# A third quad of half-size products in one batch's second MLP product, and a new order of the instructions around it

## The chip, the core and the metric

The kernel runs on one core of one Trainium2 chip. The time is the device time of one launch, in microseconds (us). One core has five engines that matter here, each with its own queue, worked off in order: TensorE for matmuls (PE in the profile), VectorE (DVE), ScalarE (ACT), GpSimd (POOL) and SyncE (SP), which issues most DMAs. Matmul results land in PSUM, in eight banks of 512 float32 for each partition; the other operands lie in SBUF.

## The reference, cut to what matters

Block-sparse attention over 4 batches, 8 heads, 768 tokens and 64 columns a head, then a residual MLP over x (4 x 768 x 512):

```
scores = q @ k.T / 8, masked by 32x32 blocks;  x = softmax(scores) @ v      # heads side by side: 512 columns
tok = w_tok @ (alpha1 * x + beta1);             u = x + lam * tok
a2 = alpha2 * u + beta2
out = u + lam * (relu(a2 @ w_ch1) @ w_ch2)      # w_ch1 512 x 2048, w_ch2 2048 x 512
```

The change concerns the last product, h = relu(a2 @ w_ch1) times w_ch2, of batch 2 alone.

## The kernel before

Pairs of heads are numbered 0 to 15, four to a batch. Each pair goes through nine score units, three of which form a **group of scores**. For a unit, PE makes the scores (`emit_qk`, matmul at L601), ACT takes the exponential (L619), DVE multiplies by the mask (`emit_keep`, L636, in the text "a mask product"), and PE multiplies by v (L671 or L648, in the text a "pv": 12 small matmuls). When a head is complete, DVE divides (L688 the reciprocal, L689 the product) into x_sb, and the two affine instructions of `emit_a1pp` (L705, L706) follow on POOL, for the last head of a batch and the last two of all on DVE.

Between these, the work of the MLPs is woven in. The order is written out by hand in strings: `W1`, `W2`, `W2L` and `W3` (L43 on; `W2L` begins at L68), one row for each group of scores, one letter for each job, and `token` (L1460) emits what a letter stands for. Instructions reach their engines' queues in that order. The letters needed here:

- q: the scores of the group's three units and the first exponential; x: the next exponential; k: a mask product; p: a pv; s: the head pair's follow-up work is made ready; Y: v is copied for the next pair.
- f: one of 32 pieces of batch 2's first MLP product (`job_f1`): four matmuls of 384 columns at L919 into a PSUM bank, then ACT's relu (L926) into hts. hts holds tokens in two chunks, tiles 0 to 2 and tiles 3 to 5.
- g: a job of the second product, from the list `P_ORDER[2]` (L1287). There are two kinds. **Direct** (`job_f2`): a tile of 128 tokens takes four jobs of four matmuls of 512 columns (L1058), then a sum into x_sb on DVE (L1067) and a store. **Quad** (`job_p`, L1187): two tiles of tokens go together and are multiplied by Strassen's scheme in Winograd's form: seven products, P1 to P7, of eight matmuls of 256 columns each (L1170), each followed by a sum into x_sb on DVE (`plus`, L1180).
- S: one of the four sums of halves of hts that a quad needs (`job_s`, L1144, a DVE instruction of 128 x 1024 bfloat16). P6 needs the second, P5 the first, P7 the third, P3 the fourth.
- W: one of eight sums of quarters of w_ch1 (`job_w`, L974, DVE), which batch 3's first product uses after all the attention. They are written into the buffer in which batch 1's output lay.
- T: a third of the token product (`job_tok2`): twelve matmuls of 256 columns at L846, a sum on DVE (L858), two casts (L865). d: a DMA transpose; v: an affine on ACT (L887); D: sums for batch 3's first product (L989).

In a quad, P1, P6 and P5 add up in one PSUM bank, and DVE takes the bank's contents into x_sb after each of the three; P7 and P4 share another bank in the same way; P2 and P3 have a bank each. PSUM is shared out by tag: `mm_tile` (L469) has three banks, `sp_tile` two pairs and `op_tile` one. A pair of `mm` banks goes to the first score unit of every group, one to every f, every T, every direct tile, and to P2, P7 and P3. P1 takes a half of an `sp` pair. A new tile takes a bank whose last user stands earlier in the written order, and its first matmul waits until that user is done.

Before the change batch 2 has two direct tiles (0 and 3) and two quads, (1, 4) and (2, 5). `W2L` has 12 rows, the attention of batch 3, pairs 12 to 15; below, "row 10" is its tenth string. Rows 6 to 12 are those that the change rewrites. `W3` follows: its first row ends pair 15 (three pvs), goes on with quad jobs and then the three T of pairs 14 and 15.

Of the kernel before, what the change touches and what calls it, by code (L numbers as in the profile page):

```python
# [18 lines left out]
B = 4  # L19
H = 8  # L20
S = 768
# [4 lines left out]
DM = 512  # L26
P = 128
NT = S // P
# [52 lines left out]
]  # L81
W3 = [
# [6 lines left out]
HN = NH // 2  # L89
# [159 lines left out]
def kernel(  # L249
# [16 lines left out]
    nc = tc.nc  # L266
# [194 lines left out]
    def sp_tile():  # L461
        return psum.tile([P, 2, 512], FP, name="sp", tag="sp", bufs=2)
# [111 lines left out]
    x_sbs = {}  # L574
# [234 lines left out]
    did = set()  # L809
# [3 lines left out]
    hts = {}  # L813
# [256 lines left out]
    def emit_store(b, o, sl, eng=nc.sync):  # L1070
        eng.dma_start(
            out[b].rearrange("(p o) n -> p o n", o=NT)[:, o, sl], x_sbs[b][:, o, sl]
        )
# [41 lines left out]
    def a_of(b, t, name, r=slice(0, HN)):  # L1115
        if name in ("X1", "X2"):
            return xs[(b, t, name)][:, r]
        c, half = {"11": (0, 0), "12": (0, 1), "21": (1, 0), "22": (1, 1)}[name]
        return hts[(b, c)][:, HN * half + r.start : HN * half + r.stop, ts(t, P)]

    SOP = {
        1: ("X1", "21", "22", ALU.add),
# [5 lines left out]
    def job_s(b, t, n, r=slice(0, HN)):  # L1128
        dst, a, c, op = SOP[n]
        rows = range(r.start, r.stop)  # L1130
        for name in (a, c):
            if name[0] == "X":
                assert all(("S", b, t, int(name[1]), m) in did for m in rows)
            else:
                h, half = divmod(int(name) - 11, 10)
                assert all(("f", b, h, HN * half + m) in did for m in rows)
# [19 lines left out]
        7: ("21", "T3", 3),  # L1156
    }
    banks = {}

    def mul(b, t, n, ps, start, cols=slice(0, HC)):  # L1160
        a, m, need = PROD[n]
        assert m in bq or all((m, r) in did for r in range(0, HN, 2))
        if need:
            assert all(("S", b, t, need, r) in did for r in range(HN))
        c, half = {"1": (0, 0), "X": (1, 0)}.get(a[0], (1, 0))
        if need == 0:
            h, half = divmod(int(a) - 11, 10)
            assert all(("f", b, h, HN * half + r) in did for r in range(HN))
        for r in range(HN):
            nc.tensor.matmul(  # L1170
                ps,
                a_of(b, t, a)[:, r],
                b_rows(m, r)[:, 0, cols],
                start=(start and r == 0),
                stop=(r == HN - 1),
                skip_group_check=True,
            )

    def plus(x, ps):
        nc.vector.tensor_tensor(out=x, in0=x, in1=ps, op=ALU.add)  # L1180

    def twice(ps):
        return ps.unsqueeze(1).broadcast_to([P, 2, HC])

    lo, hi = slice(0, HC), slice(HC, DM)

    def job_p(b, t, n):  # L1187
        x = x_sbs[b]
        last = (b, t) == (B - 1, NT // 2 - 1)
        bk = banks.setdefault((b, t), {})  # L1190
        if n in (1, 2, 7):
            bk[n] = sp_tile()[:, 0] if n == 1 else mm_tile()[:]
        if n == 3 and not last and 2 not in bk:
            bk[2] = mm_tile()[:]
        if n == 1:
            mul(b, t, 1, bk[1][:, lo], True)
            plus(x[:, t, lo], bk[1][:, lo])
        elif n == 2:
            mul(b, t, 2, bk[2][:, lo], True)
            if last or b < B - 1:  # L1200
                plus(x[:, t, lo], bk.pop(2)[:, lo])
            if last:
                emit_store(b, t, lo)
        elif n == 6:
            mul(b, t, 6, bk[1][:, lo], False)
            plus(x[:, t + 3, lo], bk[1][:, lo])
        elif n == 7:
            mul(b, t, 7, bk[7][:, lo], True)
            plus(x[:, t + 3, hi], bk[7][:, lo])
        elif n == 5:  # L1210
            mul(b, t, 5, bk[1][:, lo], False)
            plus(x[:, t : t + 4 : 3, hi], twice(bk[1][:, lo]))
        elif n == 4:
            mul(b, t, 4, bk[7][:, lo], False)
            plus(x[:, t + 3, lo], bk[7][:, lo])
            emit_store(b, t + 3, slice(0, DM))
        elif last:
            for h in range(2):
                sl = slice(HC + h * P, HC + h * P + P)
                ps = (mm_tile(), op_tile([P, DM]))[h]  # L1220
                mul(b, t, 3, ps[:, sl], True, ts(h, P))
                plus(x[:, t, sl], ps[:, sl])
                emit_store(b, t, sl, (nc.sync, nc.scalar)[h])
        else:
            sl = hi if b < B - 1 else slice(0, DM)
            mul(b, t, 3, bk[2][:, hi], b < B - 1)
            plus(x[:, t, sl], bk[2][:, sl])
            emit_store(b, t, slice(0, DM))
        did.add((b, t, n))

    NPAIR = B * NP
# [34 lines left out]
    def start_mlp(b):  # L1266
        if b == B - 1:
            todo["f"] += [
                lambda j=j: job_m(*j) if len(j) == 2 else job_f1(*j) for j in last_f1()
            ]  # L1270
        else:
            todo["f"] += [
                lambda c=c, n=n: job_f1(b, c, n) for c in range(2) for n in range(NH)
            ]
        if b not in STR:
            todo["g"] += [
                lambda o=o, g=g: job_f2(b, o, g) for o in range(NT) for g in range(4)
            ]
# [5 lines left out]
        todo["S"] += [lambda t=t, n=n, r=r: job_s(b, t, n, r) for t, n, r in S_ORDER[b]]  # L1284

    REST = (6, 7, 5, 4, 3)
    P_ORDER = {  # L1287
        2: [(0, g, "g") for g in range(4)]
        + [(t, 2) for t in (1, 2)]
        + [(3, g, "g") for g in range(4)]  # L1290
        + [(t, 1) for t in (1, 2)]
        + [(t, n) for t in (1, 2) for n in REST],
        3: [(t, n) for t in range(2) for n in (1, 2)]
        + [(t, n) for t in range(2) for n in REST]
        + [(2, n) for n in (1, 2) + REST],
    }
    ALL, R1, R2 = slice(0, HN), slice(0, HN // 2), slice(HN // 2, HN)
    S_ORDER = {
        2: [(t, n, ALL) for t in (1, 2) for n in (1, 2, 3, 4)],
        3: [(t, n, R1) for n in (1, 2, 3) for t in range(3)]  # L1300
        + [(t, n, r) for t in range(3) for n, r in ((1, R2), (2, R2), (3, R2), (4, ALL))],
    }

    def start_pair(i):
# [227 lines left out]
```

## Time and profile before

| what | us |
|---|---|
| median of 3 runs (lowest to highest) | 298.71 (298.64 to 299.35) |
| the profiled execution, whole | 298.76 |
| its span in the profile | 297.1 |
| what lies around the span | 1.66 |
| PE busy | 289.7 |
| DVE busy | 237.8 |
| ACT busy | 217.1 |
| POOL busy | 109.8 |

The granted clock of TensorE was 1.00 of full speed over the span. The profile's page gives busy times and the costliest groups of instructions. The trace answers further views: the chain of work that ended last, followed back from the last instruction and listed in order of time (start, length, engine and line); the timeline of an engine, in which "x3" means three instructions merged into one entry; and windows, which give each engine's busy time in a stretch. The ends of matmuls are modelled and overlap the next one's start, so that a matmul's price is read from start to start or from the chain, not from its own length.

### The profile page before, as it was taken

To read this page: it belongs to the slowest core of one execution; us is meant where nothing else is said; L and a number is where in the kernel's file an instruction comes from. 1 tells how busy PE (TensorE), PEld (TensorE's weight loads), DVE (VectorE), ACT (ScalarE), POOL (GpSimd) and SP (SyncE) were. 2 spreads that over 40 slices of the span, in tenths; PEclk is the share of its full clock that TensorE was granted. 3 is DMA by queue.
4 is the path that set the end of the run, shared out by engine and by line. 5 is a ranking of instruction groups with operands and counts; after the bars stand their busy time and mean duration, and the time that the engine had idled before them with its cause. 6 is when DMAs were issued, how large, how long until landed. Compare 5 with 4: busy or idle time off the path is not lost.

```text
span 297.1 us, 7554 instructions
## 1 busy us (share of the span) xinstructions
PE 289.7 (98%) x3082; PEld 193.5 (65%) x3101; DVE 237.8 (80%) x485; ACT 217.1 (73%) x324; POOL 109.8 (37%) x149
## 2 busy tenths in 40 slices
PE   8999999999999999999999999999999999999995
PEld 3688888665567565565576466556576679665884
DVE  4988899995678796977878777895956899799774
ACT  4999999998899963999779581999869744576000
POOL 8997978632443710355323340335320300000000
PEclk9999999999999999999999999999999999999999
DMA  6999999992392995729955767745520211400032
GB/s 182 184 199 186 192 171 187 171 123 44 95 147 55 112 203 84 118 65 119 125 96 73 124 110 146 103 92 69 70 62 17 38 38 29 141 1 3 0 141 73
DMA packets 57274, 31.09 MB, mean 105 GB/s; under 512 B 37204, under 2 KB 54016, under 8 KB 57240
## 3 DMA queue, kind: packets, MB, share of 16 engines
q0 software_dynamic: 16752, 14.22, 34.4%
q1 hardware_dynamic: 40020, 15.92, 29.3%
q8 instruction: 24, 0.39, 0.6%
q10 hardware_dynamic: 468, 0.47, 0.5%
q14 instruction: 10, 0.08, 0.1%
HBM read 29.75 MB, written 6.29 MB: 121 GB/s over the span
## 4 chain that ended last, share of the span: by engine, by line
PE 84%; DVE 6%; DMA 4%; ACT 3%; issue 1%; POOL 1%; SPq 0%; POOLq 0%
PE mm L919 18%; PE mm L1058 13%; PE sp L601 10%; PE mm L846 8%; PE op L671 7%; PE mm L1170 5%; PE sp L1170 4%; PE mm L601 3%; DVE eT L636 3%; PE mm L822 3%; PE op L648 2%; DMA vr<-in_v_dram 2%; ACT eT L619 2%; PE mm L1016 2%; PE sp L1016 2%; DMA uraw<-ubf 2%
## 5 line engine op out<-in xcount | busy, mean ns | idle before, releaser
L619 ACT ACTIVATE eT<-sp,expb 128x1024 f16<-128x1024 f32 x111 | 118.4, 1120 | 2.1 <-PE sp L601 1.4
L636 DVE TENSOR_TENSOR eT<-eT,mask 128x1024 f16<-128x1024 f16 x99 | 80.6, 843 | 13.5 <-ACT eT L619 13.3
L919 PE MATMUL mm<-uT,w1b 128*128 128x384 bf16 x416 | 76.8, 326 | 0.4 <-ACT hts L926 0.3
L705 POOL TENSOR_TENSOR a1pp<-x_sb,vbc 128x384 bf16<-128x384 f32 x25 | 28.5, 1138 | 119.0 <-DVE x_sb L689 84.7
L619 ACT ACTIVATE eT<-mm,expb 128x512 f16<-128x512 f32 x66 | 41.7, 685 | 26.5 <-PE mm L601 26.3
L926 ACT ACTIVATE hts<-mm 128x384 bf16<-128x384 f32 x104 | 49.1, 502 | 13.3 <-PE mm L919 12.4
L919 PEld LDWEIGHTS <-w1b 128*128 128x128 bf16 x416 | 38.7, 98 | 26.4 <-issue 2.9
L1058 PE MATMUL mm<-w2b,hts 128*128 128x512 bf16 x205 | 52.2, 379 | 0.9 <-issue 0.2
L671 PEld LDWEIGHTS <-eT 128*128 128x128 f16 x792 | 29.8, 98 | 8.8 <-issue 1.7
L1058 PEld LDWEIGHTS <-hts 128*128 128x128 bf16 x224 | 19.8, 98 | 22.3 <-issue 3.9
L671 PE MATMUL op<-vext,eT 128*128 128x65 f16 x792 | 32.1, 194 | 0.4 <-DVE x_sb L689 0.3
L601 PE MATMUL sp<-qTs,kTs 88*128 88x512 bf16 (+1 forms) x120 | 26.9, 325 | 1.2 <-ACT eT L619 0.7
L706 POOL TENSOR_TENSOR a1pp<-a1pp,vbc 128x384 bf16<-128x384 bf16 x25 | 26.7, 1069 | 2.0
L846 PE MATMUL mm<-a1pp,wtokT 128*128 128x256 bf16 x216 | 25.9, 273 | 0.1
L846 PEld LDWEIGHTS <-wtokT 128*128 128x128 bf16 x216 | 20.6, 98 | 5.6 <-issue 1.8
L1170 PEld LDWEIGHTS <-hts 128*128 128x128 bf16 x208 | 19.5, 98 | 3.0 <-issue 0.3
L858 DVE TENSOR_TENSOR x_sb<-x_sb,mm 128x512 f32<-128x512 f32 x18 | 12.3, 686 | 9.9 <-PE mm L846 9.8
L601 PE MATMUL sp<-qhT,khT 64*128 64x256 bf16 (+1 forms) x176 | 19.8, 322 | 0.0
L601 PEld LDWEIGHTS <-khT 64*128 64x128 bf16 x264 | 10.6, 94 | 12.7 <-issue 9.2
L648 PEld LDWEIGHTS <-eT 128*128 128x128 f16 x360 | 14.9, 97 | 3.8 <-issue 0.3
L689 DVE TENSOR_TENSOR x_sb<-op,rcp 128x384 f32<-128x384 f32 x28 | 15.6, 558 | 1.0
L1067 DVE TENSOR_TENSOR x_sb<-x_sb,mm 128x512 f32<-128x512 f32 x14 | 9.6, 686 | 8.2 <-PE mm L1058 6.7
(135 smaller groups left out, 376.9 us busy)
## 6 DMA issues: line engine op xcount, KB each, us to landing
out_dram<-x_sb SPq DMA_DIRECT2D x23, 256.0 KB
qpad<-in_q_dram POOLq DMA_DIRECT2D x15, 192.0 KB, 4.6
kr<-in_k_dram POOLq DMA_DIRECT2D x15, 192.0 KB, 5.3
vr<-in_v_dram POOLq DMA_DIRECT2D x15, 192.0 KB, 6.3
w1b<-in_moe_w_ch_dram POOLq DMA_DIRECT2D x4, 512.0 KB, 9.2
w2b<-in_moe_w_ch_dram POOLq DMA_DIRECT2D x4, 512.0 KB, 7.7
hts<-in_moe_w_tok_dram POOLq DMA_DIRECT2D x2, 576.0 KB, 8.7
x_sb<-in_k_dram ACTq DMA_DIRECT2D x2, 192.0 KB
```

The lines of the kernel that those rows point to most:

```text
L601: nc.tensor.matmul(sp[jj][:, dst], lhsT, rhs, start=True, stop=True, skip_group_check=True,)
L619: nc.scalar.activation(dst, at, AF.Exp, bias=expb[:], scale=SCALE)
L636: nc.vector.tensor_mul(out=e, in0=e, in1=keep)
L648: nc.tensor.matmul(op[0][:, o, :], ets[u][:, jj, h * QB + n * P : h * QB + n * P + P], vexts[i % NVB][:, w, 2 * jp + jj, :], start=op[1] == 0,
L671: nc.tensor.matmul(op[0][:, o, :], ets[u][:, jj, h * QB + n * P : h * QB + n * P + P], vexts[i % NVB][:, w, 2 * jp + jj, :], start=op[1] == 0,
L705: eng.tensor_tensor(out=dst, in0=x_sbs[b][:, :, cols], in1=bc[0], op=ALU.mult)
L706: eng.tensor_tensor(out=dst, in0=dst, in1=bc[1], op=ALU.add)
L846: nc.tensor.matmul(ps[:, o], wtokT[:, os_, ts(2 * n + o, P)], a1pps[i][:, os_, :], start=(os_ == 0 and o == 0), stop=(os_ == NT - 1 and o ...
L919: nc.tensor.matmul(ps[:, 0:QC], w1b[:, dk, ts(n, P)], uTs[b][:, dk, ts(c, QC)], start=(dk == 0), stop=(dk == 3),)
L926: nc.scalar.activation(h_row(b, c, n), ps[:, 0:QC], AF.Relu)
L1058: nc.tensor.matmul(ps[:], ht[:, nk, ts(o % 3, P)], w2b[:, nk, :], start=(nk == 0), stop=(nk == NH - 1),)
L1170: nc.tensor.matmul(ps, a_of(b, t, a)[:, r], b_rows(m, r)[:, 0, cols], start=(start and r == 0), stop=(r == HN - 1), skip_group_check=True,)
```

## The change

Batch 2's second product now has no direct tile. Its six tiles form three quads: (0, 1), whose tokens both lie in the first chunk of hts, (2, 5) and (3, 4). A quad is named by its two tiles, and `a_of`, `job_s` and `job_p` read the tiles from the name; batch 3's quads keep their pairs (t, t + 3). In the first quad, P1 takes one of the three `mm` banks, no longer half an `sp` pair, and the bank stays in use through P6 and P5, which stand in later places: P2 at the end of row 9, P1 and P6 in row 10, P5, P7 and P3 in row 11, P4 in row 12. The f's move up: at the end of row 9 one is left, where there were five before. The S's of quad (0, 1) stand in rows 7, 8 and 10 (two), those of (2, 5) in rows 11, 12 and `W3`, those of (3, 4) in `W3`. Of the W's, five move into row 6; three stay in row 7. `W3` is not changed; its g's and S's now belong to quads (2, 5) and (3, 4).

```diff
-    "q k 0 f x f p s f f x 1 L p k 2 f f f k Y f",
-    "q f L f 0 f k W W W W W W W W 1 f Y x f p g x f p f g k k 2",
-    "q x k x k Q 0 g 1 s f f g p 2 p f f k p f",
-    "q T 0 k f 1 x k f T x f 2 p k K p f",
-    "q x 0 x T k 1 k f 2 k f Q f d p L",
-    "q x 0 x K k g d k s f g f 1 k p p S S g 2",
-    "q p Y x x k g k S 0 1 k 2 g v g v g",
+    "q k 0 f x f p s f f x 1 L p k W W 2 f f f k Y W W W f",
+    "q f L f 0 f k W W W 1 f f S Y x f p f x f p f f k k 2",
+    "q x f k x f k Q 0 1 s f f p 2 p f f k S p f",
+    "q T 0 k f 1 x k f T x f 2 p k K p g",
+    "q S S g x 0 x T k g 1 k f 2 k g Q d p L",
+    "q x g 0 x K k d g k s f 1 k p p g S S 2",
+    "q p Y x x k g k S 0 1 k 2 g v g v",
...
-        c, half = {"11": (0, 0), "12": (0, 1), "21": (1, 0), "22": (1, 1)}[name]
-        return hts[(b, c)][:, HN * half + r.start : HN * half + r.stop, ts(t, P)]
+        o, half = t[int(name[0]) - 1], int(name[1]) - 1
+        return hts[(b, o // 3)][:, HN * half + r.start : HN * half + r.stop, ts(o % 3, P)]
...
+    LATE = [(2, (2, 5)), (2, (3, 4))] + [(3, (o, o + 3)) for o in range(3)]
...
     def job_p(b, t, n):
-        x = x_sbs[b]
+        x, (o1, o2) = x_sbs[b], t
...
-        if n in (1, 2, 7):
-            bk[n] = sp_tile()[:, 0] if n == 1 else mm_tile()[:]
+        if n == 1 and (b, t) in LATE:
+            bk[1] = sp_tile()[:, 0]
+        elif n in (1, 2, 7) or (n == 3 and not tail):
+            bk[n] = mm_tile()[:]
...
-        2: [(0, g, "g") for g in range(4)]
-        + [(t, 2) for t in (1, 2)]
-        + [(3, g, "g") for g in range(4)]
-        + [(t, 1) for t in (1, 2)]
-        + [(t, n) for t in (1, 2) for n in REST],
+        2: quad((0, 1), (2, 1, 6))
+        + quad((2, 5), (2,))
+        + quad((0, 1), (5, 7, 3, 4))
+        + quad((3, 4), (2,))
+        + quad((2, 5), (1,))
+        + quad((3, 4), (1,))
+        + quad((2, 5), REST)
+        + quad((3, 4), REST),
...
-        2: [(t, n, ALL) for t in (1, 2) for n in (1, 2, 3, 4)],
+        2: [(t, n, ALL) for t in ((0, 1), (2, 5), (3, 4)) for n in (1, 2, 3, 4)],
```

More of the change, by code (lines that the diff above doesn't have):

```diff
@@ L1117, in a_of, with a_ready @@
             return xs[(b, t, name)][:, r]
-        c, half = {"11": (0, 0), "12": (0, 1), "21": (1, 0), "22": (1, 1)}[name]
-        return hts[(b, c)][:, HN * half + r.start : HN * half + r.stop, ts(t, P)]
+        o, half = t[int(name[0]) - 1], int(name[1]) - 1
+        return hts[(b, o // 3)][:, HN * half + r.start : HN * half + r.stop, ts(o % 3, P)]
+    def a_ready(b, t, name, rows):
+        if name[0] == "X":
+            return all(("S", b, t, int(name[1]), m) in did for m in rows)
+        o, half = t[int(name[0]) - 1], int(name[1]) - 1
+        return all(("f", b, o // 3, HN * half + m) in did for m in rows)
     SOP = {
@@ L1130, in job_s @@
         rows = range(r.start, r.stop)
[L1131 to L1136, printed above, removed]
+        assert a_ready(b, t, a, rows) and a_ready(b, t, c, rows)
         if n == 3:
@@ L1164, in mul @@
             assert all(("S", b, t, need, r) in did for r in range(HN))
[L1165 to L1168, printed above, removed]
+        assert a_ready(b, t, a, range(HN))
         for r in range(HN):
@@ L1187, in job_p @@
     def job_p(b, t, n):
-        x = x_sbs[b]
-        last = (b, t) == (B - 1, NT // 2 - 1)
+        x, (o1, o2) = x_sbs[b], t
+        tail = b == B - 1
+        last = tail and o2 == NT - 1
         bk = banks.setdefault((b, t), {})
-        if n in (1, 2, 7):
-            bk[n] = sp_tile()[:, 0] if n == 1 else mm_tile()[:]
-        if n == 3 and not last and 2 not in bk:
-            bk[2] = mm_tile()[:]
+        if n == 1 and (b, t) in LATE:
+            bk[1] = sp_tile()[:, 0]
+        elif n in (1, 2, 7) or (n == 3 and not tail):
+            bk[n] = mm_tile()[:]
         if n == 1:
             mul(b, t, 1, bk[1][:, lo], True)
-            plus(x[:, t, lo], bk[1][:, lo])
+            plus(x[:, o1, lo], bk[1][:, lo])
         elif n == 2:
             mul(b, t, 2, bk[2][:, lo], True)
-            if last or b < B - 1:
-                plus(x[:, t, lo], bk.pop(2)[:, lo])
+            if last or not tail:
+                plus(x[:, o1, lo], bk[2][:, lo])
             if last:
-                emit_store(b, t, lo)
+                emit_store(b, o1, lo)
         elif n == 6:
             mul(b, t, 6, bk[1][:, lo], False)
-            plus(x[:, t + 3, lo], bk[1][:, lo])
+            plus(x[:, o2, lo], bk[1][:, lo])
         elif n == 7:
             mul(b, t, 7, bk[7][:, lo], True)
-            plus(x[:, t + 3, hi], bk[7][:, lo])
+            plus(x[:, o2, hi], bk[7][:, lo])
         elif n == 5:
             mul(b, t, 5, bk[1][:, lo], False)
-            plus(x[:, t : t + 4 : 3, hi], twice(bk[1][:, lo]))
+            plus(x[:, o1 : o2 + 1 : o2 - o1, hi], twice(bk[1][:, lo]))
         elif n == 4:
+            assert {(b, t, m) for m in (5, 6, 7)} <= did
             mul(b, t, 4, bk[7][:, lo], False)
-            plus(x[:, t + 3, lo], bk[7][:, lo])
-            emit_store(b, t + 3, slice(0, DM))
+            plus(x[:, o2, lo], bk[7][:, lo])
+            emit_store(b, o2, slice(0, DM))
         elif last:
@@ L1221, in job_p @@
                 mul(b, t, 3, ps[:, sl], True, ts(h, P))
-                plus(x[:, t, sl], ps[:, sl])
-                emit_store(b, t, sl, (nc.sync, nc.scalar)[h])
-        else:
[L1225 to L1228, printed above, removed]
+                plus(x[:, o1, sl], ps[:, sl])
+                emit_store(b, o1, sl, (nc.sync, nc.scalar)[h])
+        else:
+            assert {(b, t, m) for m in (1, 2, 5)} <= did
+            sl, ps = (slice(0, DM), bk[2]) if tail else (hi, bk[3])
+            mul(b, t, 3, ps[:, hi], not tail)
+            plus(x[:, o1, sl], ps[:, sl])
+            emit_store(b, o1, slice(0, DM))
         did.add((b, t, n))
@@ L1284, in start_mlp, with direct, quad @@
         todo["S"] += [lambda t=t, n=n, r=r: job_s(b, t, n, r) for t, n, r in S_ORDER[b]]
+    def direct(*tiles):
+        return [(o, g, "g") for o in tiles for g in range(4)]
+    def quad(t, order):
+        return [(t, n) for n in order]
     REST = (6, 7, 5, 4, 3)
     P_ORDER = {
-        2: [(0, g, "g") for g in range(4)]
-        + [(t, 2) for t in (1, 2)]
-        + [(3, g, "g") for g in range(4)]
-        + [(t, 1) for t in (1, 2)]
-        + [(t, n) for t in (1, 2) for n in REST],
-        3: [(t, n) for t in range(2) for n in (1, 2)]
-        + [(t, n) for t in range(2) for n in REST]
-        + [(2, n) for n in (1, 2) + REST],
+        2: quad((0, 1), (2, 1, 6))
[6 more added lines that the diff above has]
+        + quad((3, 4), REST),
+        3: quad((0, 3), (1, 2))
+        + quad((1, 4), (1, 2))
+        + quad((0, 3), REST)
+        + quad((1, 4), REST)
+        + quad((2, 5), (1, 2) + REST),
     }
     ALL, R1, R2 = slice(0, HN), slice(0, HN // 2), slice(HN // 2, HN)
+    Q3 = [(0, 3), (1, 4), (2, 5)]
     S_ORDER = {
-        2: [(t, n, ALL) for t in (1, 2) for n in (1, 2, 3, 4)],
-        3: [(t, n, R1) for n in (1, 2, 3) for t in range(3)]
-        + [(t, n, r) for t in range(3) for n, r in ((1, R2), (2, R2), (3, R2), (4, ALL))],
+        2: [(t, n, ALL) for t in ((0, 1), (2, 5), (3, 4)) for n in (1, 2, 3, 4)],
+        3: [(t, n, R1) for n in (1, 2, 3) for t in Q3]
+        + [(t, n, r) for t in Q3 for n, r in ((1, R2), (2, R2), (3, R2), (4, ALL))],
     }
```

## Prediction

> **What bounds the kernel now.** I read the page first, for the busy shares and the chain.
>
> ```profile
> PE 289.7 (98%) x3082; PEld 193.5 (65%) x3101; DVE 237.8 (80%) x485; ACT 217.1 (73%) x324; POOL 109.8 (37%) x149
> PE 84%; DVE 6%; DMA 4%; ACT 3%; issue 1%; POOL 1%; SPq 0%; POOLq 0%
> ```
>
> PE is busy 98% of the span and carries 84% of the chain, so matmul time that goes is time won, unless another engine sets the pace in the stretch where it goes. The next view is the windows, cut where the groups of scores of rows 10, 11 and 12 begin and where the first T of `W3` begins.
>
> ```profile
> core 0: us, PE busy (x) PEld busy (x) DVE busy (x) ACT busy (x) POOL busy (x), PEclk, DMA share, GB/s
> 225.25:229.70 4.45, 4.45 (x45) 3.03 (x46) 2.22 (x5) 4.43 (x8) 0.00 (x0) 1.00 0.02 4
> 229.70:235.58 5.88, 5.71 (x62) 3.88 (x64) 5.63 (x10) 4.52 (x7) 2.24 (x2) 1.00 0.34 66
> 235.58:244.07 8.49, 8.41 (x101) 5.94 (x100) 7.80 (x17) 5.10 (x6) 0.00 (x0) 1.00 0.09 33
> 244.07:255.50 11.43, 11.43 (x107) 10.24 (x108) 10.54 (x23) 4.16 (x8) 0.00 (x0) 1.00 0.23 65
> ```
>
> The second number of a row is the window's length, the third PE's busy time. In rows 11 and 12 DVE is busy 5.63 of 5.88 and 7.80 of 8.49: nearly as full as PE. The chain says the same.
>
> ```profile
> 232.78 0.34 DVE x_sb L1180
> 233.13 0.04 issue
> 233.17 0.81 PE mm L919 x4
> ...
> 236.84 0.21 DVE rcp L688
> ...
> 243.46 0.57 DVE a1pp L706
> 244.03 0.05 issue
> 244.07 4.11 PE mm L846 x36
> ```
>
> At 233.17 an f starts only when DVE has emptied the bank that it takes (a `plus` that ended at 233.12): the three `mm` banks already tie PE to DVE here. At 244.07 the first T of `W3` starts when DVE's last a1pp is done. From 236.84 to there the chain runs on DVE alone, one instruction after another, 7.23 us. After 244.07 PE is busy without a gap.
>
> **The price of the matmuls**, from other pieces of the chain, where PE runs back to back:
>
> ```profile
> 181.43 1.31 PE mm L846 x12
> 182.74 1.73 PE mm L1058 x8
> ...
> 197.13 0.43 PE sp L601 x4
> ...
> 198.97 0.36 PE op L671 x12
> ...
> 248.18 0.87 PE sp L1170 x8
> ...
> 269.04 0.65 PE mm L919 x4
> ```
>
> A T is 1.31, a pv 0.36, an f 0.65, a quad's product 0.87, a job of a direct tile half of 1.73. The scores of a group are 0.76 (the four of 0.43 and some 0.33 for the rest). The change removes two direct tiles, 2 x 4 x 0.865 = 6.92, and adds 7 x 0.87 = 6.10: **0.82 less on PE**. In rows 6 to 9 the work stays the same (four direct jobs go, 3.46; four f's and P2 come, 2.60 + 0.87), so the whole 0.82 is in rows 10 to 12. The Trainium skill, page "TensorE: Matmul & The Clock Gate", section "Back-to-back issue gap", gives a sustained 131 ns for a matmul of 512 columns and 81 ns for 128; with some 98 ns for 256 in between, an estimate, the direct tiles would cost 4.2 and the quad 5.5, and the change would lose 1.3 on PE. The rows above (216 and 109 ns) fit that section's other formula, N/2.4 + 2.5 ns, and so speak for the 0.82.
>
> **What it puts on DVE.** Four sums S (0.68 each), seven plus instead of two: about 3.8 us more before 244, in a queue that is nearly full there. To see what is late, I follow PE and DVE through rows 10 to 12 in the new order. These rows give the starts and the steps:
>
> ```profile
> 225.17 0.39 PE L601 MATMUL mm<-qhT,khT 64*128 64x512 bf16 x2
> 225.92 1.48 PE L846 MATMUL mm<-a1pp,wtokT 128*128 128x256 bf16 x12
> 229.66 0.46 PE L601 MATMUL mm<-qhT,khT 64*128 64x512 bf16 x2
> 235.51 0.39 PE L601 MATMUL mm<-qhT,khT 64*128 64x256 bf16 x4
> ```
>
> ```profile
> 227.44 0.69 DVE L858 TENSOR_TENSOR x_sb<-x_sb,mm 128x512 f32<-128x512 f32 x1 [2.22 <-PE mm L846]
> ...
> 228.58 1.89 DVE L636 TENSOR_TENSOR eT<-eT,mask 128x1024 f16<-128x1024 f16 x3
> ...
> 230.61 0.56 DVE L689 TENSOR_TENSOR x_sb<-op,rcp 128x384 f32<-128x384 f32 x1
> 231.38 1.41 DVE L636 TENSOR_TENSOR eT<-eT,mask 128x1024 f16<-128x1024 f16 x1 [0.21 <-ACT eT L619]
> 232.71 0.41 DVE L1180 TENSOR_TENSOR x_sb<-x_sb,mm 128x256 f32<-128x256 f32 x1
> 233.04 1.07 DVE L636 TENSOR_TENSOR eT<-eT,mask 128x1024 f16<-128x1024 f16 x1
> ```
>
> A T that starts at 225.92 ends at 227.23; DVE starts its sum 0.21 later, and with its two casts needs 1.14 (227.44 to 228.58). A mask product costs 0.60 from start to start (three in 1.89, the last 0.69 long), a plus 0.33 (232.71 to 233.04; 0.41 till it ends), the plus of P5, over 512 columns, as much as a mask product. From DVE to PE go 0.04 (233.13 to 233.17). Before, row 10 took 4.49 (225.17 to 229.66), row 11 5.85, row 12 with the head of `W3` 8.56 (235.51 to 244.07): 18.90.
>
> *Row 10.* P1 holds one of three `mm` banks until P5's plus in row 11. The other two go in turn to T, f and P2 of (2, 5); row 11's first unit needs both, so its scores wait for the plus of that P2. PE gets to T's end after scores, P1 and T: 0.76 + 0.87 + 1.31 = 2.94. Behind that, DVE has T's sum and casts, a mask product, P6's plus, two mask products and the awaited plus: 0.21 + 1.14 + 0.60 + 0.33 + 0.60 + 0.60 + 0.41 + 0.04 = 3.93. PE has only P6, f, P2 and a pv: 0.87 + 0.65 + 0.87 + 0.36 = 2.75. Row 10 takes 6.87, and **PE stands 1.2 us**. DVE itself stands idle ahead of T's sum, so the S's of this row cost nothing.
>
> *Row 11.* P7 holds a bank and row 12's first unit needs the other two; one was P3's. P5 ends at 0.76 + 0.87 = 1.63; then DVE has P5's plus, a mask product, P7's plus, two mask products, P3's plus: 0.21 + 0.60 + 0.60 + 0.33 + 0.60 + 0.60 + 0.41 + 0.04 = 3.39, in all 5.0. The exponentials leave it at that:
>
> ```profile
> 230.08 1.27 ACT L619 ACTIVATE eT<-mm,expb 128x512 f16<-128x512 f32 x2
> 231.23 2.12 ACT L619 ACTIVATE eT<-sp,expb 128x1024 f16<-128x1024 f32 x2
> ```
>
> The last ends 3.69 after the row's scores began (233.35 against 229.66), and with its mask product and P3's plus comes to 4.7. But the mask products can be slower beside POOL:
>
> ```profile
> 231.24 1.00 POOL L705 TENSOR_TENSOR a1pp<-x_sb,vbc 128x384 bf16<-128x384 f32 x1 [10.51 <-DVE x_sb L689]
> 232.32 1.25 POOL L706 TENSOR_TENSOR a1pp<-a1pp,vbc 128x384 bf16<-128x384 bf16 x1
> ```
>
> The two that began inside these ended 0.55 after POOL's end (232.24 to 232.79, 233.57 to 234.11), as if POOL kept them out. The same two POOL instructions follow the division that ends row 10's list, so they reach 3.1 us into row 11, over the first mask product (2.44): 0.5 more. The Trainium skill, page "SBUF — State Buffer", section "SBUF: two separate sides", calls this an exclusive lock between GpSimd and a DVE instruction with two SBUF inputs, held for the whole instruction. The two rows agree; by the lock row 11 takes 5.5, without it 5.0. I take 5.2, since POOL's start hangs on my own row 10. PE alone would need 0.76 + 2 x 0.87 + 2 x 0.36 + 0.87 = 4.09: **PE stands 1.1**.
>
> *Row 12.* DVE's list from 236.84 to 244.07 changes by one sum of 512 (0.60) that becomes two plus (0.66). PE's share shrinks by 0.87, but T still waits for the last a1pp at the end of this list: 8.56 as before, and PE's gain turns into idle time ahead of T.
>
> *Before row 10.* Row 8 has f's directly behind its first two exponentials, where direct jobs stood. The fourth f wants the first one's bank. Its relu comes behind two exponentials:
>
> ```profile
> 211.41 0.39 PE L601 MATMUL mm<-qhT,khT 64*128 64x512 bf16 x2
> ...
> 211.83 1.27 ACT L619 ACTIVATE eT<-mm,expb 128x512 f16<-128x512 f32 x2 [0.69 <-PE mm L601]
> 212.99 2.12 ACT L619 ACTIVATE eT<-sp,expb 128x1024 f16<-128x1024 f32 x2
> ```
>
> The relu is done 1.58 (to 212.99) + 1.0 + 0.4 = 3.0 into the row, PE arrives after 0.76 + 3 x 0.65 = 2.71: 0.3 lost (0 if ACT starts earlier). The W's in row 6 stand ahead of mask products whose pv is five or more f's away; these f's cover them. They write where batch 1's output was, so they wait for its last store. The trace shows that store's issue and the mask product that the first W now follows, 4.4 us later; its landing isn't shown. I take no wait (up to 0.5).
>
> ```profile
> 195.81 0.33 SPq L1071 DMA_DIRECT2D out_dram<-x_sb  x1
> ...
> 200.08 0.68 DVE L636 TENSOR_TENSOR eT<-eT,mask 128x1024 f16<-128x1024 f16 x1
> ```
>
> After T, PE and DVE have the same list as before, so nothing is made up.
>
> **The sum.** 6.87 + 5.2 + 8.56 = 20.63 against 18.90: 1.73 later, with row 8's 0.3 about 2.0. The profiled execution took 298.76 (0.05 above the median of the runs): **300.8 us, slower**, because a PSUM bank kept through two groups makes PE wait for DVE, which costs 2.6 where 0.82 is saved.
>
> **The rivals.**
> - *PE stays the bound* (the other side). Both banks come back in time: rows 10 and 11 are PE's 5.69 and 4.09, and row 12 PE's list too, some 7.5: 17.3 against 18.9, so 297.2, faster. It decides at one point: DVE must come from T's end to P2's plus in under 2.75. Seven steps of 0.33 to 1.14 in a row speak against it. For it: rows 10 and 11 lose some 0.6 now, behind ACT's relus, of which the new order has four less there. 6 in 100.
> - *The banks are covered, DVE's list in row 12 is not*: 5.69 + 4.09 + 8.56 = 18.34, 0.56 less, and row 8's 0.3 more: 298.5, no change. 12 in 100.
> - *Only one of the two bank waits comes*, because row 10's list is shorter than I add it up: 5.69 + 5.0 + 8.56 = 19.25, so 299.1, with row 8 299.4, up to 300.0. 15 in 100.
> - *The W's wait for the store as well*, DVE stands in front of everything: 0.5 and more on top, 301.3 to 301.8. 5 in 100.
>
> **How the numbers follow.** The forecast, 300.0 to 301.3, has 62 in 100. 299.0 to 301.8 takes in the third and fourth rival and holds some 82. A measurement can tell 0.3% (0.9 us) from no change: faster (under 297.8) has the first rival's 6, slower (over 299.6) the forecast, the last and some half of the third, 75, the same what is left, 19.
>
> **What would show it.** In the chain, PE's scores at the head of rows 11 and 12 (mm L601) follow a DVE plus (L1180), with PE idle some 1 us each; PE's busy time falls by about 0.8 while the span grows; DVE waits for PE at T's sum in row 10; the first mask product of row 11 is longer than 0.69; T in `W3` starts near 246 and follows L706. I am wrong if the waits of mm L601 on L1180 stay under 0.3 us, or if the end moves though T does not.

## The result, and the profile after

| | before | after |
|---|---|---|
| median of 5 runs (lowest to highest) | 298.70 (298.62 to 299.35) | 300.84 (300.30 to 301.43) |
| ratio to before, 95% interval | | 1.0077 [1.0062, 1.0091] |
| the profiled execution, whole | 298.76 | 300.3 |
| its span | 297.1 | 298.6 |

The changed kernel is 2.1 us slower. The page of its profile gives the busy times and the chain's shares by engine; the granted clock is as before.

```profile
PE 290.4 (97%) x3125; PEld 195.6 (66%) x3125; DVE 241.6 (81%) x494; ACT 217.0 (73%) x324; POOL 109.8 (37%) x149
...
PE 92%; DVE 5%; ACT 1%; issue 0%
```

PE's share of the chain went up and DVE's went down, although the kernel is slower: the chain before ran through a DMA and ACT for 4% and 3%, this one hardly. Shares over the whole span don't answer the question; the rows do. The windows, cut at the starts of rows 10, 11, 12 and of the first T of `W3`, are those of the prediction's second fence, with the changed kernel's times:

```profile
225.01:231.90 6.89, 6.20 (x62) 4.72 (x62) 5.75 (x13) 4.42 (x6) 0.00 (x0) 1.00 0.18 35
231.90:237.09 5.19, 4.48 (x57) 3.48 (x56) 3.98 (x9) 2.73 (x4) 1.92 (x2) 1.00 0.17 33
237.09:245.59 8.50, 7.79 (x103) 6.44 (x103) 8.26 (x18) 5.10 (x6) 0.00 (x0) 1.00 0.18 64
```

Row 10 takes 6.89, row 11 5.19, row 12 with the head of `W3` 8.50: 20.58 where it was 18.90, so 1.68 more. From there to the end of the span both kernels need the same: 297.1 - 244.07 = 53.03 before, 298.6 - 245.59 = 53.01 after. PE's timeline shows what the three starts waited for (in brackets: the idle time and its releaser):

```profile
230.82 0.39 PE L601 MATMUL mm<-qhT,khT 64*128 64x512 bf16 x1
231.90 0.37 PE L601 MATMUL mm<-qhT,khT 64*128 64x512 bf16 x1 [0.69 <-DVE x_sb L1179]
...
236.10 0.28 PE L601 MATMUL mm<-qhT,khT 64*128 64x256 bf16 x1
237.09 0.38 PE L601 MATMUL mm<-qhT,khT 64*128 64x256 bf16 x3 [0.70 <-DVE x_sb L1179]
...
245.59 0.61 PE L846 MATMUL mm<-a1pp,wtokT 128*128 128x256 bf16 x4 [0.45 <-DVE a1pp L706]
```

The first unit of a group wants two `mm` banks. One is free, so a first score runs at 230.82; the second has to wait until 231.90 for a `plus` (now L1179). Rows 11 and 12 are counted from this second score. The chain shows why the `plus` is late:

```profile
226.82 1.32 PE mm L846 x12
...
228.16 0.70 DVE x_sb L858
...
228.89 0.49 DVE ubf L865 x2
229.38 0.60 DVE eT L636
229.98 0.33 DVE x_sb L1179
230.31 1.21 DVE eT L636 x2
231.52 0.34 DVE x_sb L1179
231.86 0.04 issue
231.90 0.28 PE mm L601
```

From the end of T (228.14) to 231.86 DVE works off eight instructions in a row (T's sum, two casts, a mask product, P6's `plus`, two mask products, P2's `plus`), and only the last gives back the bank.

**Rows 6 to 9** hold the rest of the loss: from row 6's start to row 10's 28.91 (196.10 to 225.01) against 28.43 before (196.74 to 225.17), 0.48 more. It lies in row 8:

```profile
210.99 0.56 PE L601 MATMUL mm<-qhT,khT 64*128 64x512 bf16 x2
211.22 0.77 PE L601 MATMUL sp<-qhT,khT 64*128 64x256 bf16 x6
211.92 3.07 PE L919 MATMUL mm<-uT,w1b 128*128 128x384 bf16 x16
214.82 0.90 PE L671 MATMUL op<-vext,eT 128*128 128x65 f16 x24
```

The sixteen matmuls of four f's take 2.90 from 211.92 to 214.82, where 4 x 0.65 = 2.60 is their price: 0.30 lost, in the last f, which the chain of this stretch lets wait for a relu.

```profile
212.05 1.70 ACT eT L619 x2
213.75 0.39 ACT hts L926
214.14 0.04 issue
214.18 0.81 PE mm L919 x4
```

The other 0.17 is in the scores: 0.93 from 210.99 to 211.92, where the group's price is 0.76.

Together 0.48 + 1.68 = 2.16 from row 6 to T, which is the 2.14 between the medians. The two profiled spans are only 1.5 apart: the after kernel's profiled execution began row 6 at 196.10 and before's at 196.74, though nothing ahead of row 6 was changed. Over the profiles below this start lies anywhere from 196.10 to 197.38. So the single executions of this kernel scatter by more than some of the edits below bring, and I read those from the rows: the changed kernel's own runs lie between 300.30 and 301.43, so a difference of 0.3 to 0.5 between two medians doesn't stand by itself.

### The profile page after: what moved, and what is told of

It reads as the page before. It is cut to its first block, busy times and chain, and to the rows that moved or that the text cites. A ratio compares the mean times of both kernels' runs of the same rounds, so it can differ in the third digit from the quotient of the medians.

```text
span 298.6 us, 7630 instructions
## 1 busy us (share of the span) xinstructions
PE 290.4 (97%) x3125; PEld 195.6 (66%) x3125; DVE 241.6 (81%) x494; ACT 217.0 (73%) x324; POOL 109.8 (37%) x149
## 4 chain that ended last, share of the span: by engine, by line
PE 92%; DVE 5%; ACT 1%; issue 0%
PE mm L919 22%; PE mm L1058 14%; PE sp L601 11%; PE mm L846 8%; PE op L671 8%; PE mm L1169 6%; PE mm L601 4%; PE sp L1169 4%; PE mm L822 3%; PE op L648 2%; PE mm L1016 2%; PE sp L1016 2%; DVE eT L636 2%; PE mm L648 1%; PE op L481 1%; DVE x_sb L1179 1%
## 5 line engine op out<-in xcount | busy, mean ns | idle before, releaser
L636 DVE TENSOR_TENSOR eT<-eT,mask 128x1024 f16<-128x1024 f16 x99 | 78.9, 824 | 11.2 <-ACT eT L619 11.0
L1058 PE MATMUL mm<-w2b,hts 128*128 128x512 bf16 x192 | 46.8, 380 | 0.0
L1058 PEld LDWEIGHTS <-hts 128*128 128x128 bf16 x192 | 16.9, 98 | 19.4 <-issue 3.6
L1169 PEld LDWEIGHTS <-hts 128*128 128x128 bf16 x248 | 23.2, 98 | 3.2 <-issue 0.3
L601 PE MATMUL sp<-qhT,khT 64*128 64x512 bf16 (+1 forms) x176 | 20.2, 323 | 0.0
L858 DVE TENSOR_TENSOR x_sb<-x_sb,mm 128x512 f32<-128x512 f32 x18 | 12.3, 686 | 8.5 <-PE mm L846 8.5
L601 PE MATMUL mm<-qhT,khT 64*128 64x512 bf16 (+1 forms) x88 | 13.7, 330 | 1.4 <-DVE x_sb L1179 1.4
```

Source lines behind the costliest of these rows:

```text
L601: nc.tensor.matmul(sp[jj][:, dst], lhsT, rhs, start=True, stop=True, skip_group_check=True,)
L636: nc.vector.tensor_mul(out=e, in0=e, in1=keep)
L1058: nc.tensor.matmul(ps[:], ht[:, nk, ts(o % 3, P)], w2b[:, nk, :], start=(nk == 0), stop=(nk == NH - 1),)
L1169: nc.tensor.matmul(ps, a_of(b, t, a)[:, r], b_rows(m, r)[:, 0, cols], start=(start and r == 0), stop=(r == HN - 1), skip_group_check=True,)
```

## The experiments

All ratios are to the kernel before, which was measured beside each of them (medians of 298.59 to 298.70). The rows' lengths are read as above (rows 10 / 11 / 12 with the head of `W3`; 4.49 / 5.85 / 8.56 before, 6.89 / 5.19 / 8.50 after).

**1. The W's alone.** The kernel before, with the eight W's where the change has them.

```diff
-    "q k 0 f x f p s f f x 1 L p k 2 f f f k Y f",
-    "q f L f 0 f k W W W W W W W W 1 f Y x f p g x f p f g k k 2",
+    "q k 0 f x f p s f f x 1 L p k W W 2 f f f k Y W W W f",
+    "q f L f 0 f k W W W 1 f Y x f p g x f p f g k k 2",
```

> The kernel before with the eight sums W of w_ch1's quarters at the changed kernel's places (five in row 6, three in row 7) and nothing else. My account gives them no price: DVE idles there and the f's cover the mask products behind them, so rows 6 to 10 keep their 28.4 us and the time is that of before, 298.7 within 0.2. Rival: the W's are what made rows 6 to 9 0.5 us longer in the changed kernel (28.9 from row 6's scores to row 10's); then 299.2 here.

298.66, ratio 1.0002 [0.9989, 1.0016]. The window from row 6 to row 10:

```profile
196.53:224.96 28.43, 28.32 (x276) 17.52 (x278) 21.67 (x38) 23.21 (x40) 10.01 (x10) 1.00 0.39 69
```

The same window of the kernel before:

```profile
196.74:225.17 28.43, 28.33 (x276) 17.52 (x278) 20.80 (x38) 23.24 (x40) 9.81 (x10) 1.00 0.42 68
```

Both take 28.43. DVE is busy 0.87 more with the W's moved, and PE doesn't notice: the W's cost nothing, and all of the change's loss belongs to the quad and its order.

**2. P5 in row 10.** The bank of P1 is given back a row sooner, and P2 of (2, 5) takes P5's place in row 11.

```diff
-        2: quad((0, 1), (2, 1, 6))
+        2: quad((0, 1), (2, 1, 6, 5))
         + quad((2, 5), (2,))
-        + quad((0, 1), (5, 7, 3, 4))
+        + quad((0, 1), (7, 3, 4))
```

> The changed kernel with P5 of quad (0, 1) directly behind P6, so that P1's bank comes back in row 10 and isn't kept through a group of scores. If keeping the bank were the cause, the waits of PE at the heads of rows 11 and 12 (together 2.2 us) would go, and the time would fall to about 298.8. If DVE's list behind T's sum is the cause and the bank only the place where it shows, P5 itself waits for P6's plus, P3's plus and the last a1pp come at nearly the same time, and the first T of W3 starts 0.1 to 0.2 earlier: 300.6.

300.55, ratio 1.0065 [1.005, 1.008]; rows 6.68 / 5.18 / 8.50. The second score of row 11 now waits for nothing, yet row 10 is only 0.21 shorter. PE's timeline has the wait in another place:

```profile
230.90 1.03 PE L1169 MATMUL mm<-qTs,xs 128*128 128x256 bf16 x8 [0.72 <-DVE x_sb L1179]
```

P5 adds into the bank that DVE still has to empty of P6, and P6's `plus` stands behind T's sum, two casts and a mask product. The bank that was held through two groups was not the cause by itself; what PE waits for is DVE's list, at whichever instruction needs it first.

**3. Less work on DVE ahead of the list.** S3 and S4 of quad (0, 1), in row 10, left out, in `S_ORDER[2]` too (the diff shows the row alone). P7 and P3 of this quad then multiply the halves unsummed, with as many matmuls as before.

```diff
-    "q S S g x 0 x T k g 1 k f 2 k g Q d p L",
+    "q g x 0 x T k g 1 k f 2 k g Q d p L",
```

> The changed kernel without the third and fourth sum S of quad (0, 1) (both in row 10): P7 and P3 of that quad take the halves unsummed, so two tiles of the output are not the reference's. DVE has 1.2 us less to do. If DVE's load as such sets the time, it falls by 1.2, to 299.6. By my account DVE does these sums while it waits for T in row 10: rows 10, 11 and 12 keep 6.9, 5.2 and 8.5 us and the time stays at 300.8.

300.86, ratio 1.0088 [1.0059, 1.0118]. Row 10:

```profile
225.32:232.21 6.89, 6.20 (x62) 4.73 (x62) 4.54 (x11) 4.42 (x6) 0.00 (x0) 1.00 0.17 35
```

DVE does 1.21 less (4.54 against 5.75) and the row is as long as before. DVE stands idle ahead of T's sum anyway (0.89 in the changed kernel); work taken away there only widens the idle time.

**4. Less work on DVE within the list.** The two casts behind this T's sum go to ACT.

```diff
-        copy = nc.scalar.copy if i >= NPAIR - 2 else nc.vector.tensor_copy
+        copy = nc.scalar.copy if i >= NPAIR - 2 or (i >= NPAIR - 4 and sl.start == 4) else nc.vector.tensor_copy
```

> The changed kernel with the two casts behind T's sum in row 10 on ACT instead of DVE (0.41 us of DVE time, inside the list that P2's plus stands behind; ACT is idle there). By the list, row 10 falls from 6.9 to 6.45 us, rows 11 and 12 stay, and the time falls by 0.4, to 300.4. If the bank kept through the groups sets the pace by itself, nothing changes: 300.8.

300.33, ratio 1.0059 [1.0042, 1.0076]; rows 6.36 / 5.19 / 8.50.

```profile
225.66:232.02 6.36, 6.19 (x62) 4.72 (x62) 5.25 (x11) 4.61 (x8) 0.00 (x0) 1.00 0.15 30
```

The row is shorter by 0.53, the 0.49 of the casts that the chain above shows and an issue, and the median is 0.5 lower. Half a microsecond of DVE counts in full behind T's end, and 1.21 counts for nothing ahead of it.

**5. Row 12's list.** S3 of quad (2, 5) left out of row 12 and of `S_ORDER[2]` (the diff shows the row alone).

```diff
-    "q p Y x x k g k S 0 1 k 2 g v g v",
+    "q p Y x x k g k 0 1 k 2 g v g v",
```

> The changed kernel without the third sum S of quad (2, 5), which stands in row 12 (P7 of that quad takes the half unsummed, so two tiles of the output are not the reference's). By my account row 12 and the head of W3 are DVE's list, 8.5 us: without this sum of 0.6 it is shorter by 0.4 (the row's last mask product then waits for its exponential), 8.1, and the time falls by 0.4, to 300.4. Rows 10 and 11 keep 6.9 and 5.2. If DVE's load as such counted, this would bring what the two sums of row 10 bring, 0.6 for each. If PE set row 12's pace, nothing would change.

300.35, ratio 1.0058 [1.0044, 1.0072]; rows 6.89 / 5.18 / 7.99.

```profile
237.35:245.34 7.99, 7.62 (x103) 6.40 (x103) 7.74 (x17) 5.10 (x6) 0.00 (x0) 1.00 0.19 68
```

Here DVE's list is full (7.74 of 7.99), and 0.5 of the 0.60 taken out of it comes back at the end, 0.1 more than I expected.

**6 to 8. Row 11's wait: does it count?** The prediction added the three stands up. But DVE's timeline has hardly a gap from P5's `plus` at 233.72 to the last a1pp, so the stand ahead of row 12 could be the same time as the list behind it. *Run 6* takes P3 ahead of two pvs and a mask product; *run 7* moves the first S of (2, 5) to DVE's idle time at the head of row 11; *run 8* does both. The diffs stand in this order.

```diff
-    "q x g 0 x K k d g k s f 1 k p p g S S 2",
+    "q x g 0 x K k d g k g s f 1 k p p S S 2",
...
-    "q x g 0 x K k d g k s f 1 k p p g S S 2",
+    "q S x g 0 x K k d g k s f 1 k p p g S 2",
...
-    "q x g 0 x K k d g k s f 1 k p p g S S 2",
+    "q S x g 0 x K k d g k g s f 1 k p p S 2",
```

> Row 11 of the changed kernel with its third g (P3 of quad (0, 1)) one mask product and two pvs sooner. If the length of DVE's list behind P5 sets row 11, P3's plus comes 0.6 sooner and row 11 takes 4.6 where it took 5.19. What that brings to the end divides two theories. If the two stands add up, as the prediction added them, row 12 with the head of W3 stays at 8.50, the first T of W3 comes 0.6 sooner and the time is about 0.6 lower (some 300.2). If DVE's list is one from P5's plus (233.72 in the changed kernel) to the last a1pp (245.55), the mask product and the two S that were ahead of row 12's start only move behind it: row 12 takes 9.1, T comes when it came, and the time is that of the changed kernel (300.8). I expect the second, since DVE stands idle only 0.04 to 0.1 between 233.72 and 245.55.

> The first S of quad (2, 5) moves from the end of row 11 to its head, where DVE stands idle 1.18 (232.55 to 233.72). If DVE's list from P5's plus to the last a1pp is one and has nothing else to wait for, taking 0.6 out of it brings T 0.6 sooner (about 300.2). If PE's scores and pv at the head of row 12 (done 1.3 after row 12 begins, at 238.38, with the reciprocal waiting for it at 238.40) hold the list as well, S only leaves a gap there and nothing moves (300.8, row 12 8.50). I expect the second.

> Both edits together: P3 sooner and the first S in DVE's idle time. If row 12's start (held by P3's plus) and DVE's list are two limits of nearly the same length, either edit alone brings nothing and both bring the whole: row 11 4.6, row 12 with the head of W3 8.5, T 0.6 sooner, time 300.2. If the stands simply add up, this gives the same as the earlier P3 alone. If POOL's a1pp keeps the moved S waiting, row 11 is some 0.3 longer than 4.6 and the gain is 0.3.

Run 6: 300.58, ratio 1.0064 [1.0045, 1.0084]. PE's timeline, rows 11 and 12 and the T:

```profile
232.25 0.37 PE L601 MATMUL mm<-qhT,khT 64*128 64x512 bf16 x1 [0.70 <-DVE x_sb L1179]
...
236.45 0.75 PE L601 MATMUL mm<-qhT,khT 64*128 64x256 bf16 x4
236.95 0.68 PE L601 MATMUL sp<-qhT,khT 64*128 64x512 bf16 x4
...
245.80 1.38 PE L846 MATMUL mm<-a1pp,wtokT 128*128 128x256 bf16 x11 [0.45 <-DVE a1pp L706]
```

The 0.70 of idle time ahead of row 12 is gone; its `sp` scores come 4.70 after row 11's start (232.25 to 236.95), where they came 5.31 after it (231.90 to 237.21 in the changed kernel): 0.6 sooner, as expected. T comes 13.55 after row 11's start, 13.69 in the changed kernel: only 0.14 of the 0.6 reaches the end. So the stand of row 11 was not a loss of its own that could be taken away alone: behind it the same list of DVE went on.

Run 7: 301.32, ratio 1.0088 [1.0064, 1.0112], T 14.07 after row 11's start (232.72 to 246.79): 0.38 *later* than in the changed kernel, which neither theory had. POOL's timeline and DVE's:

```profile
233.45 1.38 POOL L705 TENSOR_TENSOR a1pp<-x_sb,vbc 128x384 bf16<-128x384 f32 x1 [12.28 <-DVE x_sb L689]
234.90 0.92 POOL L706 TENSOR_TENSOR a1pp<-a1pp,vbc 128x384 bf16<-128x384 bf16 x1
```

```profile
233.28 0.68 DVE L1145 TENSOR_TENSOR xs<-hts 128x1024 bf16<-128x1024 bf16 x1
...
235.15 1.22 DVE L636 TENSOR_TENSOR eT<-eT,mask 128x1024 f16<-128x1024 f16 x1
```

In the changed kernel the same instructions read:

```profile
232.63 0.99 POOL L705 TENSOR_TENSOR a1pp<-x_sb,vbc 128x384 bf16<-128x384 f32 x1 [12.28 <-DVE x_sb L689]
233.70 0.92 POOL L706 TENSOR_TENSOR a1pp<-a1pp,vbc 128x384 bf16<-128x384 bf16 x1
```

```profile
233.72 0.69 DVE L1179 TENSOR_TENSOR x_sb<-x_sb,mm 128x512 f32<-128x512 f32 x1 [1.18 <-PE mm L1169]
234.33 0.84 DVE L636 TENSOR_TENSOR eT<-eT,mask 128x1024 f16<-128x1024 f16 x1
```

With the S under way on DVE, POOL's first instruction takes 0.39 longer (1.38 against 0.99; 1.37 in run 8, where the S stands at the same place), POOL ends so much later, and DVE's mask product, which ends 0.55 after POOL both times (235.82 to 236.37, 234.62 to 235.17), is 0.38 longer. That is the whole 0.38; the S itself, taken out of the list behind P5, brought nothing, since DVE now stands 0.76 ahead of row 12's reciprocal, waiting for a pv. P5's `plus`, which reads one of its inputs from PSUM, takes 0.69 beside the same POOL instruction, as long as the other sums of 512 columns. So the two engines share something that an S and a mask product need, and the idle time of DVE was not free.

Run 8: 300.43, ratio 1.0058 [1.0039, 1.0077]; T 13.47 after row 11's start (232.09 to 245.56), 0.22 sooner than in the changed kernel. Against run 7 it is 14.07 - 13.47 = 0.60 sooner: P3's 0.6 comes through whole once the list behind it is shorter, and 0.38 of it pays for POOL. The expectation's third theory has the size (0.3) but the delay the wrong way round: the S is not kept waiting, it is what makes POOL late. Alone, P3's move brought 0.14 and the S's, without POOL's 0.38, nothing; so two limits of nearly the same length end together here, the start of row 12's scores and DVE's list.

**9. Row 8's relu.** The exponential and the f behind it change places.

```diff
-    "q x f k x f k Q 0 1 s f f p 2 p f f k S p f",
+    "q f x k f x k Q 0 1 s f f p 2 p f f k S p f",
```

> The changed kernel with row 8's first f ahead of its second exponential, so that this f's relu stands behind one exponential instead of two. By my account the fourth f of the row then finds its bank free: row 8 falls from 6.98 to 6.7 us, the rows behind it stay, and the time falls by 0.3, to 300.5. Rival: the loss in row 8 is made up later, since rows 10 to 12 wait for DVE anyway; then 300.8.

301.25 (300.64 to 301.44), ratio 1.0082 [1.0066, 1.0097]: not the 0.3 expected, and within the range of the changed kernel's own runs. Its profiled execution started row 6 later than any other, at 197.38, and the edit comes only behind that; whether the other three runs did so too isn't known. Row 8 of this kernel:

```profile
212.27 0.56 PE L601 MATMUL mm<-qhT,khT 64*128 64x512 bf16 x2
212.49 0.77 PE L601 MATMUL sp<-qhT,khT 64*128 64x256 bf16 x6
213.19 2.77 PE L919 MATMUL mm<-uT,w1b 128*128 128x384 bf16 x16
215.81 0.90 PE L671 MATMUL op<-vext,eT 128*128 128x65 f16 x24
216.54 1.63 PE L919 MATMUL mm<-uT,w1b 128*128 128x384 bf16 x8
218.01 0.53 PE L671 MATMUL op<-vext,eT 128*128 128x65 f16 x12
```

The four f's take 2.62 (213.19 to 215.81), so the relu's 0.30 is gone. The next two take 1.47 (216.54 to 218.01) where 1.30 is their price: 0.17 came back. Row 6 to T is 49.36 against 49.49 in the changed kernel. The prediction's cause of the 0.3 is right, but a plain swap wins only 0.13, less than the scatter between executions.

**10 to 12. Is a third quad worth anything without the waits?** *Three* is the changed kernel with rows 6 to 12, `P_ORDER[2]` and `S_ORDER[2]` set anew, so that no `mm` bank waits for a long list of DVE: f's stand in rows 10 and 11, and seven of the ten products of rows 6 to 12 in row 12. *Two* is the kernel before with the same rows set anew by the same rule. *Three_y* is *three* with the copy of pair 15's v (Y) moved from row 7 (where it stood ahead of the first x behind 1) to the end of row 8. First the rows of *three_y* with its lists of products and sums, then those of *two* with its products; only the new lines are shown.

```diff
+    "q f k 0 x p f s f f x f 1 L p k W W 2 f k Y W W W f f",
+    "q f L 0 k W f W W 1 x f f p x p f k f k S f f 2",      # three: "1 Y x"
+    "q x g k x k Q 0 f S 1 f s p 2 p k f p Y",
+    "q T 0 k 1 x f f k T x f 2 p k S K p",
+    "q x 0 x T k S 1 f f k f 2 k Q d p L f",
+    "q f x 0 x K k g d k s f 1 k p f p g 2",
+    "q S S f p g S Y x x g k g k g 0 1 k g 2 v v g g",
...
+        2: [((0, 1), 2), ((0, 1), 1), ((0, 1), 6), ((0, 1), 5), ((3, 4), 2), ((0, 1), 7), ((0, 1), 3), ((2, 5), 2), ((2, 5), 1), ((3, 4), 1), ((0, 1), 4), ((2, 5), 7), ((2, 5), 6), ((2, 5), 5), ((3, 4), 6), ((2, 5), 4), ((3, 4), 7), ((3, 4), 5), ((2, 5), 3), ((3, 4), 4), ((3, 4), 3)],
...
+        2: [(t, n, ALL) for t, n in [((0, 1), 1), ((0, 1), 3), ((0, 1), 2), ((0, 1), 4), ((2, 5), 1), ((2, 5), 2), ((2, 5), 3), ((3, 4), 1), ((3, 4), 2), ((3, 4), 3), ((3, 4), 4), ((2, 5), 4)]],
```

```diff
+    "q k f 0 x p s f f f x 1 L f p k f f f 2 f k Y",
+    "q L 0 k W W W W W W W W 1 Y f f x f p f x p k g f k f 2 g",
+    "q x k x k Q 0 g 1 s f g p f 2 f p k p",
+    "q T 0 k f 1 x k f T x 2 p k f K p",
+    "q x f f 0 x T k 1 k 2 f k f Q d p L",
+    "q f g x 0 x f f K k d f k s 1 S k p S p 2",
+    "q g p S Y x x g k g k 0 1 g k 2 v g g v",
...
+        2: [(0, 0, 'g'), (0, 1, 'g'), (0, 2, 'g'), (0, 3, 'g'), (2, 2), (1, 2), (3, 0, 'g'), (3, 1, 'g'), (1, 1), (1, 7), (3, 2, 'g'), (2, 1), (1, 6), (3, 3, 'g'), (1, 5), (1, 4), (2, 6), (1, 3), (2, 7), (2, 5), (2, 3), (2, 4)],
```

> The three quads of the changed kernel, with f, g, S, W in rows 6 to 12 set anew so that DVE's list behind T's sum in row 10 is short: quad (0, 1) is spread over rows 8 to 12, more f's are left for rows 9 to 12, where ACT and DVE have room, and only a1pp of the last head stands close to the first T of W3. If the third quad is worth its 0.82 us of PE wherever DVE's list covers it, and the waits around it go as well, PE has no wait over 0.2 us in rows 10 to 12 and the time is 1.0 to 1.4 below that of before: 297.3 to 297.7. If a third quad costs more on DVE than it saves on PE in any order, it is 299 or more.

> The kernel before, two direct tiles and two quads, with the same freedom: f, g, S, W in rows 6 to 12 set anew. Only the waits of before go (some 0.6 us in rows 10 to 12): 298.1 to 298.3. The distance to the three quads set anew is the third quad's own worth, 0.8. If the gain of the other kernel were the new order alone, this one would be as fast.

> The three quads set anew, with one letter moved: the copy of pair 15's v (Y) from row 7 to the end of row 8. In the run without this move DVE stood at that copy until the load of v landed at 209.85, and PE lost 0.67 + 0.28 us in row 8. If that wait is all that was left, PE runs without one from row 6 to the first T of W3 (46.3 us from row 6's scores to T, against 47.2 with the wait and 47.3 before) and the time is 297.0 to 297.4. If the third quad can't be covered by DVE in any order, it stays at 298.0.

*Three*: 298.0, ratio 0.9982 [0.997, 0.9994], 0.3 more than the expectation's upper end. Its chain:

```profile
204.29 5.55 DMA vr<-in_v_dram
...
209.87 0.37 DVE vext L329
```

DVE reached the copy of pair 15's v before the load had landed (209.85) and stood there with everything behind it; PE then lost 0.67 and 0.28 in row 8. *Three_y* puts that right: 297.16 (296.90 to 297.49), ratio 0.9951 [0.9938, 0.9963], faster than both kernels. *Two*: 298.19, ratio 0.999 [0.998, 1.0], as expected. From row 6 to T the windows of *two* and of *three_y* have PE busy in every moment:

```profile
196.41:243.15 46.74, 46.74 (x482) 30.79 (x481) 36.03 (x69) 37.35 (x60) 12.07 (x12) 1.00 0.29 51
```

```profile
196.54:242.49 45.95, 45.95 (x506) 32.86 (x505) 41.36 (x77) 36.99 (x60) 12.26 (x12) 1.00 0.28 52
```

The third quad is worth 46.74 - 45.95 = 0.79 here, 1.0 between the medians, which were measured apart. And the same stretch of the kernel before and of the changed one:

```profile
196.74:244.07 47.33, 46.98 (x478) 30.45 (x480) 36.50 (x68) 37.29 (x60) 12.05 (x12) 1.00 0.31 56
```

```profile
196.10:245.59 49.49, 47.25 (x505) 33.07 (x505) 40.33 (x76) 37.32 (x60) 11.80 (x12) 1.00 0.27 52
```

The changed kernel and *three_y* have the same matmuls (505 and 506 records). In one they are "busy" 47.25, in the other 45.95. So 1.30 of the changed kernel's busy time is no work: short waits between matmuls that the view merges, and the modelled ends before each stop. Of row 8's 0.48, for one, the view shows only 0.14 as idle (6.84 of 6.98 busy). Measured against *two* and *three_y*, the kernel before stands 47.33 - 46.74 = 0.59 from row 6 to T and the changed one 49.49 - 45.95 = 3.54; 3.54 - 0.59 - 0.79 is the 2.16 found above.

## Why the prediction was right, point by point

- **The total**: 300.8 forecast, 300.84 measured; +2.0 forecast against the profiled execution, +2.16 measured from row 6 to T and +2.14 between the medians. The parts fit less closely than the whole: rows 10 to 12 cost 1.68 where 1.73 was forecast, rows 6 to 9 cost 0.48 where 0.3 was. The last sentence of the sum, 2.6 of stands where 0.82 is saved, would give 1.8 and not 2.0: it leaves out PE's stand ahead of T and the stands that the kernel before had already. By the runs it is 3.54 against 0.59.
- **0.82 less on PE**: right, 0.79 between *two* and *three_y*. In the changed kernel it can't be seen, and the sign that I named for it failed: PE's busy time did not fall by 0.8 but rose from 289.7 to 290.4. Of that, 0.27 lies from row 6 to T (46.98 to 47.25): 0.79 less work, but 1.30 of busy time that is no work where the kernel before has 46.98 - 46.74 = 0.24. The other 0.48 (193.47 to 193.95) lies ahead of row 6, where nothing was changed; there the trace of the kernel before holds 16 matmul records fewer.
- **Row 10, 6.87**: 6.89. Shown by runs 2 to 4: DVE's list behind T's end sets it, neither the bank as such nor DVE's load. So the list that I added up was right, and the cause that I put in front, "a PSUM bank kept through two groups", was too narrow: given back a row sooner, the bank brought 0.21. PE's idle time reads 0.69 and not 1.2, since a first score slips into the free bank; from that score to the next pass 1.08.
- **Row 11, 5.2 between 5.0 and 5.5**: 5.19, by the steps as added up but for one: from P5's `plus` to P7's 1.37 (233.72 to 235.09) instead of 1.20, because POOL held the mask product up. I had allowed 0.5 for that; POOL's second instruction took 0.92 and not 1.25, so the price was some 0.17. That the 5.2 hits is luck: it was a value between two cases, neither of which came. That a mask product or an S and POOL's a1pp hold each other up is shown by runs 7 and 8, in both directions, which bears out the rule of the Trainium skill that the prediction named ("SBUF — State Buffer", section "SBUF: two separate sides").
- **The stands add up**: this step was right in the sum and wrong as a mechanism. Run 6 removed the stand of row 11, and 0.14 of its 0.6 came through, since from P5's `plus` to T one list of DVE sets the end as well; with the S out of that list the 0.6 came through whole (run 8 against run 7). So the stand could not be taken away by itself, as the sum would have it.
- **Row 12 with the head of `W3`, 8.56**: 8.50; run 5 shows that it is DVE's list.
- **Row 8's 0.3**: right in place, cause and size (0.30; run 9). Left out were 0.17 in the scores of this row. They stand behind three relus of row 7's f's on ACT in the timeline; that these are the cause I did not test.
- **The W's cost nothing**: right (run 1), so their wait for the store, the last rival, did not come. The trace puts the mask product ahead of the first W 4.3 behind the store's issue (195.81 to 200.08), not 4.4. The first rival's mechanism, PE as the bound, is what *three_y* shows, with another order.

## What to carry to other kernels

Fewer matmul cycles help only where the results' way out keeps pace: ahead of cutting PE work, write down for each PSUM bank which instruction of another engine gives it back and what stands in front of that instruction in its queue. The length of that list, not the engine's load, is the price: 1.21 us taken from DVE ahead of it brought nothing, 0.5 within it brought 0.5. Where two limits of the same length stand one behind the other, loosening one shows little or nothing, so loosen both, or put independent matmuls (here f's) between the dependent ones, before giving the idea up.

## What the runs showed of the hardware

- DVE and POOL hold each other up where an a1pp on POOL meets a DVE instruction with both inputs in SBUF: beside an S the a1pp went from 0.99 to 1.38, and a mask product begun beside an a1pp ended 0.55 after POOL (0.84 in the changed kernel, 1.22 in run 7). P5's `plus`, with one input in PSUM, kept its 0.69 beside the same a1pp. So an idle gap of DVE beside a busy POOL isn't free.
- "Busy" PE time of the same matmuls differed by 1.30 of 46 us between two orders, at the same granted clock.
- The instructions ahead of row 6, the same in all these kernels, took 196.1 to 197.4 us from one profiled execution to another, more than most of these edits moved.
